# A planner's constants changed in a fused attention and gated-product kernel: a short wait for one engine, more places for raw weights, larger margins

## The chip, the cores and the metric

The kernel runs on one core of one Trainium2 chip. The metric is the device time of one execution in microseconds (us), as the median of several runs. A profile is one further execution, recorded by the hardware profiler.

## The reference

```python
# q, k, v: (8 batches, 8 heads, 576 tokens, 64); omega: (128, 64)
phi(x): h = x @ omega.T - sum(x*x)/2;  return exp(h - max(h)) / sqrt(128)     # x scaled by 64**-0.25
kv  = phi(k).T @ v;  z = sum over tokens of phi(k)
x   = (phi(q) @ kv) / (phi(q) @ z + 1e-6)                                      # -> (4608, 512)
out = ((x @ w_a) * (x @ w_b)) @ w_out                                          # w_a, w_b: 512 x 1536, w_out: 1536 x 512
```

q, k, v and omega are float32, the three weights come as float64.

## The kernel before

The work is cut by batch (8 of 576 tokens, of which 512 are the batch's main part; the 64 left over of every batch are gathered into a ninth block). For a batch there are four attention units, one for each pair of heads (`pair(u, gate)`, u = 4 * batch + pair), and then one block of gated products over 12 slices of the inner size 1536. A full-precision product is made of three passes over operands that are split into a high and a low part. Batches 0 and 1 use `moe_block` (L819 forms pa and pb, L774 forms the output o), the later blocks `moe_block7` (L909), which saves an eighth of the products with sums of weights that are made once, during batch 1, and kept in DRAM (`td`, `bd`).

Before the first block can run, the weights must be turned from 64-bit into two 32-bit parts. There are 36 weight units (for each slice one of w_a, one of w_b, one of w_out). For a unit, SyncE (SP) issues a load of 512 KB into a tile called `raw`; ACT runs two conversions on it (L319, L321); DVE joins them (L323); ACT or DVE makes the high part (L268 or L270), DVE the low part (L276). `raw` has a ring of two places of its own, raw0 and raw1. The first 18 units (n < 18) may also use the ten places in `late[:10]`, places of weights that are converted last and so are empty so far. The converted weights of slice i sit in 24 places w0..w11 and u0..u11.

No engine's order is the order in the source. `Graph` collects every operation with its dependencies, an estimate of its time, a priority (lower is earlier) and a `margin`; `schedule` then plays the whole program through on these estimates and writes down the order in which each engine is to work. On the chip the engines keep that order, whatever is late, and wait on semaphores. `need` is the earliest planned start: the end of the dependencies, a latency (70 ns, 150 ns more behind TensorE), plus `margin`, and not before `at` (for the conversion of unit n, 28000 + 2600 n ns). For every engine the planner takes the operation with the smallest key:

```python
o.need = max(t + o.margin, o.at)
...
key = (max(s, free[e] + 30), o.prio, o.n)
```

where `s` is the operation's earliest start and `free[e]` the time at which the engine is free. An operation that could start later than another that is ready loses, whatever the priorities are. Priorities: attention of pair u has 1000 u and a little more, so that the first batch lies below 4000; the conversion of unit n has 4000 + 111 n; copies and products of the block on DVE and ACT have -10.

In the first batch's attention (`tok_tail`) TensorE forms pn (L716), DVE adds, inverts, scales (`rd` L722 and L724, `x32t` L725, `tails` L729), twice for a pair, and TensorE transposes the result into px (L736). For most pairs of the later batches (27 in all) q' is scaled on ACT, transposed by DVE in blocks of 32 (`qd`), stored to DRAM by four DMAs (`qdr`, L633) and loaded back as `hq`; the load has `margin=CFG["BACK"]`. SP issues nearly all DMAs, in the planned order, and waits in that order.

Of the kernel before, what the change touches and what calls it, by code (L numbers as in the profile page):

```python
# [18 lines left out]
B, H, S, D, M = 8, 8, 576, 64, 128  # L19
# [14 lines left out]
SQ = (0.5 / float(D) ** 0.5) ** 0.5  # L34
EPS = 1e-6 * M

CFG = dict(FAST=(0, 1, 2, 3), JOIN0=False, WARM=8, HROOM=["w0", "u1", "w1", "u2", "w2", "u3"], H=3, TURN=(7,), BACK=300, AT=2, GATES=(-3, -1, 1, 3), SQPE=4, MARGIN=1200, LOAD=2500, SUMS=1000, JOIN=(0, 1, 2), CONV=(28000, 2600))

# [14 lines left out]
class Graph:  # L55
# [75 lines left out]
    def schedule(self, bw=330.0, dma_lat=2000):  # L131
        engines = ("PE", "ACT", "DVE", "POOL", "SP")
        free = dict.fromkeys(engines, 0)
        dma_free = 0
        after, left = {}, {}
        for o in self.ops:
            left[o] = len(o.deps)
            for d in o.deps:
                after.setdefault(d, []).append(o)
        ready = {e: [] for e in engines}  # L140

        def enter(o):
            t = 0
            for d in o.deps:
                same = d.eng.keys() == o.eng.keys() == {"PE"}
                t = max(t, d.end + (0 if same else self.LAT + (150 if "PE" in d.eng else 0)))
            o.need = max(t + o.margin, o.at)
            for e in o.eng:
                ready[e].append(o)

        for o in self.ops:
            if not left[o]:
                enter(o)
        done = []
        while len(done) < len(self.ops):
            best = None
            for e in engines:
                mine = None
                for o in ready[e]:
                    at = self.place(o) if o.alloc else (0, ())  # L160
                    if at is None:
                        continue
                    s = max(free[e], o.need, at[0])
                    for x in o.eng:
                        if x != e and max(free[x], o.need, at[0]) + o.eng[x] <= s + o.eng[e] - (o.eng[e] <= o.eng[x]):
                            break
                    else:

                        key = (max(s, free[e] + 30), o.prio, o.n)
                        if mine is None or key < mine[0]:  # L170
                            mine = key, s, o, at[1]
                if mine and (best is None or mine[1] < best[1]):
                    best = (*mine, e)
            if best is None:
                stuck = [o for e in engines for o in ready[e]]
                raise RuntimeError(f"stuck at {len(done)} of {len(self.ops)}: " + ", ".join(
                    f"{[b.name for b in o.alloc]}" for o in stuck[:12]))
            _, s, o, got, e = best
            o.start = s
            if o.bytes:  # L180
                free[e] = s + o.eng[e]
                begin = max(s, dma_free)
                dma_free = begin + o.bytes / bw
                o.end = dma_free + dma_lat
            else:
                o.end = s + o.eng[e]
                free[e] = max(s + 30, o.end - self.OVER[e])
            o.eng = {e: o.eng[e]}
            for b, slot in got:
                b.slot = slot  # L190
                self.slots[slot] = b
                self.rings[b.ring]["at"] += 1
            for r in ready.values():
                if o in r:
                    r.remove(o)
            done.append(o)
            for n in after.get(o, ()):
                left[n] -= 1
                if not left[n]:
                    enter(n)  # L200
        self.order = sorted(done, key=lambda o: (o.start, o.n))
        return self.order
# [11 lines left out]
def dve(n):  # L214
    return 150 + 1.04 * n


def act(n):
    return 165 + 0.86 * n
# [11 lines left out]
def tile_attention_moe(ctx: ExitStack, tc: tile.TileContext, kqt, kqtt, kqn, kqnt, vx, omst, idn, wab, wout, out):  # L231
    nc = tc.nc
    SQPE = CFG["SQPE"]
    const = ctx.enter_context(tc.tile_pool(name="const", bufs=1))
# [5 lines left out]
    def f(ap):  # L240
        return ap.bitcast(F32)

    g = Graph()
    for name, n in dict(X=2, Xw=0, nat=2, x2=0, v=2, h=CFG["H"], qd=1, kvz=1, sm=3, sq=3, ht=2, Xt=1, xl=0, xts=2, rd=2, x=4, xa=2, xf=2, S=2, st=0,
                        w=NF, u=NF, t=0, tst=0, wo=3, raw=2, a=2, c=0, bq=0, ghl=2, osb=0, zs=1, z2=1, zb=1, k2=1, kl=2, dn=1, tails=1, zr=1,
                        at=CFG["AT"], ab=2, o=4).items():
        g.ring(name, n)
# [16 lines left out]
    def copier(o, i, scale=None):  # L264

        def go(e):
            if e == "ACT":
                nc.scalar.copy(o(), i())  # L268
            elif e == "DVE":
                nc.vector.tensor_copy(o(), i())  # L270
            else:
                nc.gpsimd.tensor_scalar(o(), i(), 1.0, 0.0, op0=ALU.mult, op1=ALU.add)
        return go
# [13 lines left out]
    for k in range(4):  # L287
        g.op({"POOL": 110}, lambda e, k=k: nc.gpsimd.memset(ind.ap[D * (k // 2):D * (k // 2) + D, D * (k % 2):D * (k % 2) + D], float(k in (0, 3))),
             w=[(ind, k)], prio=-5000)
# [5 lines left out]
    def nothing(e):  # L295
        for _ in range(CFG["WARM"]):
            nc.tensor.matmul(none.ap[:], zero.ap[:], zero.ap[:, 0:1].to_broadcast([P, SM]), start=True, stop=True)
# [11 lines left out]
    def convert(raw, hi, lo, hb, n, pr, at):  # L309

        wd = (lambda: raw.ap.bitcast(I32).rearrange("p (n t) -> p n t", t=2)) if wide else None
        if wide:
            top, low = (lambda: wd()[:, :, 1]), (lambda: wd()[:, :, 0])

            g.op({"ACT": act(n) + 60}, lambda e: nc.scalar.activation(f(top()), f(top()), AF.Prelu, scale=2.0 ** -112, alpha=-2.0 ** 32),  # L319
                 r=[(raw, 1)], w=[(raw, 1)], prio=pr, at=at)  # L320
            g.op({"ACT": act(n) + 60}, lambda e: nc.scalar.activation(low(), low().bitcast(U32), AF.Copy, scale=2.0 ** -29 * 15 / 16),  # L321
                 r=[(raw, 0)], w=[(raw, 0)], prio=pr, at=at)
            g.op({"DVE": dve(n)}, lambda e: nc.vector.scalar_tensor_tensor(  # L323
                low(), top(), 3, low(), op0=ALU.logical_shift_left, op1=ALU.bitwise_or),
                r=[(raw, None)], w=[(raw, 0)], prio=pr, at=at)
            src = lambda: f(low())
        else:
            src = lambda: raw.ap[:, 0:n]
        g.op({"ACT": act(n) + 60, "DVE": 160 + 0.52 * n}, copier(hi, src), r=[(raw, 0)], w=[(hb, 0)], prio=pr, at=at, alloc=[hb])
        g.op({"DVE": dve(n)}, subber(lo, src, hi), r=[(raw, 0), (hb, 0)], w=[(hb, 1)], prio=pr, at=at)  # L330
# [5 lines left out]
    late = [f"{r}{k}" for k in range(NF - 1, -1, -1) for r in "uw"]  # L336
    for n, (kind, i, w) in enumerate(units):
        pr = 4000 + n * 4000 / len(units)
        more = late[:10] if n < 18 else []
        raw = g.buf("raw", [P, NW], I64 if wide else F32, f"raw{n}", more)  # L340
        src = (wab[i, w] if kind == "ab" else wout[i])
        g.op({"SP": 330}, dma(lambda raw=raw: raw.ap[:], lambda src=src: src), w=[(raw, None)], alloc=[raw], prio=pr - 600,
             nbytes=P * NW * (8 if wide else 4))
        if kind == "ab":
            hb = wab_b[i, w] = g.buf("wu"[i % 2], [P, 2, NC4, P], F32R, f"w{'ab'[w]}{i}")
            v = lambda hb, k: hb.ap[:, k].rearrange("p c f -> p (c f)")
        else:
            hb = wo_b[i] = g.buf("wo", [P, 2, E], F32R, f"wo{i}")
            v = lambda hb, k: hb.ap[:, k]
        convert(raw, lambda hb=hb, v=v: v(hb, 0), lambda hb=hb, v=v: v(hb, 1), hb, NW, pr, CFG["CONV"][0] + n * CFG["CONV"][1])  # L350
        if kind == "o":
            db = g.buf(None, None, None, f"wod{i}")
            wo_store[i] = db
            g.op({"SP": 330}, dma(lambda i=i: wod[i], lambda hb=hb: f(hb.ap)), r=[(hb, None)], w=[(db, None)], prio=pr + 600,
                 nbytes=P * 2 * E * 4)
# [75 lines left out]
    def square_sums(src, sq, n, nm, pr, b, alloc_sq):  # L431

        for nat, o, part in src:
            g.op({"ACT": act(n * D)}, lambda e, nat=nat: nc.scalar.activation(nat.ap[:], nat.ap[:], AF.Square, scale=SQ),
                 r=[(nat, None)], w=[(nat, None)], prio=pr, margin=0 if b < 2 else CFG["LOAD"])
            g.op({"DVE": dve(n * D)}, lambda e, nat=nat, o=o: nc.vector.tensor_reduce(o(), nat.ap[:], axis=X, op=ALU.add),
# [532 lines left out]
    for b in range(B + 1):  # L969
        if b < B1:  # L970
            moe_block(b)
        else:
            if b == B:

                for hp in range(NHP):
# [3 lines left out]
                         prio=-20, nbytes=P * SM * 4)  # L979
# [78 lines left out]
```

## Time and profile before

| what | us |
|---|---|
| median of 3 runs | 1091.68 |
| lowest and highest of them | 1089.23, 1092.51 |
| the profiled execution's own time | 1093.12 |
| its span from first to last instruction | 1091.3 |

The profiled execution took 1.8 us more than its span, and 1.4 us more than the median of the runs. In what follows PE is TensorE's matmul, PEld its weight load, DVE VectorE, ACT ScalarE, POOL GpSimd, SPq SyncE's DMA issues. A row of a timeline has the start, the duration, engine, line and operation, output<-input, and in brackets how long the engine was idle before it and what ended that. PE's busy time holds slow matmuls too: a matmul at a granted clock of 0.5 counts double.

### The profile page before, as it was taken

The numbers are of one execution on the slowest core, as the hardware profiler recorded it, in microseconds if no ns is written. First come the engines' busy times: TensorE is split into PE (matmuls) and PEld (weight loads), VectorE is DVE, ScalarE is ACT, GpSimd is POOL, SyncE is SP. The second block draws the span as 40 slices with busy tenths as digits, with TensorE's granted clock in tenths as the row PEclk, the third lists the DMA queues.
The fourth block names the chain that finished last, engine by engine and source line by source line (L and its number), as shares of the span: only waits on it lengthen the run. The fifth ranks groups of instructions, "written<-read, shape, count | busy, mean of one in ns | idle before, by whom it ended". The sixth has DMA issues, their size and how long they took to land.

```text
span 1091.3 us, 21360 instructions
## 1 busy us (share of the span) xinstructions
PE 1071.8 (98%) x7725; PEld 928.2 (85%) x7725; DVE 802.7 (74%) x1975; ACT 575.5 (53%) x1557; POOL 102.9 (9%) x176
## 2 busy tenths in 40 slices
PE   8999899999999999999999999999999999999998
PEld 7877677777779888988888989888898989999997
DVE  5899687889897778777696888777876766456544
ACT  6987667767674556564565566464645412002001
POOL 0011111111010111110111111010101100000000
PEclk9989999999999999999999999999999999999999
DMA  9656765798779788978889798888786798777773
GB/s 360 231 201 189 247 226 192 260 324 300 260 280 364 266 285 307 322 275 287 279 289 324 258 301 279 311 278 290 262 306 225 251 288 284 243 241 256 258 233 88
DMA packets 113209, 292.45 MB, mean 268 GB/s; under 512 B 16208, under 2 KB 33360, under 8 KB 113104
## 3 DMA queue, kind: packets, MB, share of 16 engines
q1 hardware_dynamic: 112496, 290.44, 78.4%
q8 instruction: 61, 1.00, 0.4%
q10 hardware_dynamic: 608, 0.66, 0.2%
q14 instruction: 44, 0.36, 0.1%
HBM read 242.61 MB, written 48.43 MB: 267 GB/s over the span
## 4 chain that ended last, share of the span: by engine, by line
PE 83%; DVE 6%; DMA 4%; ACT 3%; issue 1%; SPq 0%; ACTq 0%; DVEq 0%
PE p L909 37%; PE o L774 25%; PE ppk L449 5%; PE pb L819 4%; PE pa L819 4%; PE pkv L584 3%; PE pm L643 2%; DMA out_dram<-osb 1%; DMA raw<-in_wab_dram 1%; ACT hq L615 1%; DVE raw L323 1%; DVE sm L470 1%; DMA td<-ts 1%; DVE c L919 1%; DMA hq<-qdr 1%
## 5 line engine op out<-in xcount | busy, mean ns | idle before, releaser
L774 PE MATMUL o<-wo,ghl 128*128 128x512 f32 x1296 | 352.7, 400 | 0.3 <-ACT osb L268 0.2
L919 DVE TENSOR_TENSOR c<-p,c 128x512 f32<-128x512 f32 (+1 forms) x336 | 208.1, 619 | 141.8 <-PE p L909 139.5
L774 PEld LDWEIGHTS o<-wo,ghl 128*128 128x128 f32 x1296 | 225.7, 189 | 41.3 <-ACT osb L268 0.7
L909 PE MATMUL p<-S,t 128*128 128x256 f32 x1512 | 208.8, 283 | 0.7 <-ACT c L268 0.7
L909 PEld LDWEIGHTS p<-S,t 128*128 128x128 f32 x1512 | 195.7, 190 | 9.3 <-ACT c L268 1.5
L551 POOL TENSOR_TENSOR z<-hk 128x256 f32<-128x256 f32 x56 | 44.2, 789 | 714.9 <-ACT hk L482 684.0
L482 ACT ACTIVATE hk<-hk,sm 128x128 f32<-128x128 f32 x192 | 63.1, 394 | 56.1 <-DVE sm L478 53.9
L268 ACT COPY c<-p 128x256 f32<-128x256 f32 x84 | 31.0, 369 | 109.8 <-PE p L909 105.6
L615 ACT ACTIVATE hq<-hq,dn 128x128 f32<-128x128 f32 x224 | 70.3, 395 | 33.4 <-DVE dn L611 32.7
L268 ACT CAST ghl<-c 128x512 fp32r<-128x512 f32 x54 | 33.3, 621 | 92.0 <-DVE c L954 90.4
L605 DVE CUSTOM_DVE_ANT_0 junk<-hq,zb 128x128 bf16<-128x128 f32 x224 | 65.2, 291 | 17.8 <-ACT zb L268 15.6
L449 PEld LDWEIGHTS ppk<-om,X 64*128 64x128 f32 x512 | 61.9, 188 | 18.7 <-issue 6.2
L449 PE MATMUL ppk<-om,X 64*128 64x128 f32 x512 | 74.0, 285 | 2.6 <-DVE x L276 2.3
L819 PE MATMUL pb<-x,wb 128*128 128x512 f32 x288 | 76.3, 405 | 0.0
L909 PEld LDWEIGHTS p<-x,t 128*128 128x128 f32 x504 | 70.3, 189 | 6.8 <-DVE c L919 0.3
L449 PE MATMUL ppq<-om,X 64*128 64x128 f32 x512 | 73.7, 285 | 0.7 <-ACT kl L268 0.7
L819 PE MATMUL pa<-x,wa 128*128 128x512 f32 x288 | 74.0, 401 | 0.0
L909 PE MATMUL p<-S,bq 128*128 128x256 f32 x504 | 73.9, 282 | 0.0
L909 PE MATMUL p<-x,t 128*128 128x256 f32 x504 | 73.9, 282 | 0.0
L909 PEld LDWEIGHTS p<-x,wb 128*128 128x128 f32 x504 | 65.4, 188 | 4.3 <-DVE zr L276 0.3
L909 PEld LDWEIGHTS p<-x,wa 128*128 128x128 f32 x504 | 65.1, 188 | 4.3 <-DVE c L919 0.6
L909 PE MATMUL p<-x,wb 128*128 128x256 f32 x504 | 68.1, 282 | 0.0
(158 smaller groups left out, 1713.1 us busy)
## 6 DMA issues: line engine op xcount, KB each, us to landing
t<-td SPq DMA_DIRECT2D x168, 512.0 KB, 5.2
wo<-wod SPq DMA_DIRECT2D x96, 512.0 KB, 5.3
bq<-bd SPq DMA_DIRECT2D x84, 256.0 KB, 5.4
X<-in_kqt_dram SPq DMA_DIRECT2D x31, 512.0 KB, 5.5
qdr<-qd SPq DMA_DIRECT2D x108, 144.0 KB, 3.5
hq<-qdr SPq DMA_DIRECT2D x27, 576.0 KB, 6.6
raw<-in_wab_dram SPq DMA_DIRECT2D x24, 512.0 KB, 5.0
td<-ts SPq DMA_DIRECT2D x24, 512.0 KB, 5.5
```

The lines of the kernel that those rows point to most:

```text
L268: nc.scalar.copy(o(), i())
L449: nc.tensor.matmul(pps[w].ap[:, c * M:c * M + M], x()[rows, c * P:c * P + P], om.ap[rows], start=True, stop=True)
L482: g.op({"ACT": 392}, lambda e, c=c, w=w: nc.scalar.activation(dst[w].ap[:, c], src[w](c), AF.Exp, scale=SC, bias=sm.ap[:, 2, w, c:c + 1]), ...
L551: g.op({"POOL": pool2(n)}, lambda e: ENG[e].tensor_tensor(o(), a(), c(), op=ALU.add), r=r, w=w, alloc=list(al), prio=pri)
L584: nc.tensor.matmul(pkv.ap[D * j:D * j + D, 0:M], vb.ap[:, vc, 0:D], c(), start=(n == 0), stop=(n == 4))
L605: g.op({"DVE": 413}, lambda e, c=c, j=j, rr=rr, qc=qc: nc.vector.tensor_tensor_reduce(out=junk.ap[rr], in0=qc(), in1=zb.ap[rr, j], scale=1 ...
L615: g.op({"ACT": 392}, lambda e, c=c, src=src: nc.scalar.activation(hq.ap[:, c], src(), AF.Copy, scale=dn.ap[:, c:c + 1]), r=[sd, (dn, None) ...
L643: nc.tensor.matmul(pm.ap[D * j:D * j + D], kl.ap[:, j], qT[1](j), start=True, stop=True)
L774: nc.tensor.matmul(po.ap[:], ghl.ap[:, gi, t * P:(t + 1) * P], wo.ap[:, wi], start=(n == 0 and i == 0), stop=(n == NF - 1 and i == 2))
L819: nc.tensor.matmul(pb.ap[:], wt.ap[:, wi, c], xs[c].at(xi), start=(c == 0 and i == 0), stop=(c == NC4 - 1 and i == 2))
L909: nc.tensor.matmul(pb.ap[:, half], wcol(wi, c), xc(xi, c), start=n == 0, stop=n == 5)
L919: g.op({"DVE": dve(n)}, lambda e: nc.vector.tensor_tensor(c4.ap[:, o], pb.ap[:, half], y(), op=ALU.add), r=[*((pb, k) for k in range(half. ...
```

## The change

Four constants of the plan change. DVE's key may treat an operation of the first batch's attention (priority 0 to 4000) that can start up to 150 ns after DVE is free as if it were ready, so that its priority decides. The two ACT conversions of a raw tile get a margin of 2000 ns behind the planned landing of its load. The margin of the load of q' goes from 300 to 1500 ns. And raw tiles of units 18 to 23 may use six further places, of units 24 to 29 three, of units 30 to 32 one, where they had only raw0 and raw1. The instructions are the same; their order, the places and the waits follow from a new plan.

```diff
-CFG = dict(FAST=(0, 1, 2, 3), ... BACK=300, ... CONV=(28000, 2600))
+CFG = dict(WAIT=150, RAW=2000, FAST=(0, 1, 2, 3), ... BACK=1500, ... CONV=(28000, 2600))
...
-                        key = (max(s, free[e] + 30), o.prio, o.n)
+                        wait = CFG["WAIT"] if e == "DVE" and 0 <= o.prio < 4000 else 0
+                        key = (max(s - wait, free[e] + 30), o.prio, o.n)
...
             g.op({"ACT": act(n) + 60}, lambda e: nc.scalar.activation(f(top()), f(top()), AF.Prelu, scale=2.0 ** -112, alpha=-2.0 ** 32),
-                 r=[(raw, 1)], w=[(raw, 1)], prio=pr, at=at)
+                 r=[(raw, 1)], w=[(raw, 1)], prio=pr, at=at, margin=CFG["RAW"])
             g.op({"ACT": act(n) + 60}, lambda e: nc.scalar.activation(low(), low().bitcast(U32), AF.Copy, scale=2.0 ** -29 * 15 / 16),
-                 r=[(raw, 0)], w=[(raw, 0)], prio=pr, at=at)
+                 r=[(raw, 0)], w=[(raw, 0)], prio=pr, at=at, margin=CFG["RAW"])
...
-        more = late[:10] if n < 18 else []
+        more = late[:10] if n < 18 else late[:6] if n < 24 else late[:3] if n < 30 else late[:1] if n < 33 else []
```

## Rows read from the trace of the kernel before

**Rows 1.** The page's head and its first part: busy us, share, instructions.
```profile
span 1091.3 us, 21360 instructions
...
PE 1071.8 (98%) x7725; PEld 928.2 (85%) x7725; DVE 802.7 (74%) x1975; ACT 575.5 (53%) x1557; POOL 102.9 (9%) x176
```
**Rows 2.** TensorE's waits, whole span: engine, line, releaser: us, times, longest.
```profile
PE px L736 <- DVE x32t L725: 3.1, 1, 3.1
PE pk L594 <- ACT hk L482: 2.8, 1, 2.8
PE ppk L449 <- DVE x L276: 2.3, 2, 2.0
PE pm L643 <- DMA hq<-qdr: 1.0, 1, 1.0
...
PE ppq L449 <- ACT kl L268: 0.7, 1, 0.7
...
PE o L774 <- ACT osb L268: 0.2, 1, 0.2
```
**Rows 3.** Windows: length, PE, PEld, DVE, ACT, POOL busy, PEclk, DMA share, GB/s.
```profile
56.30:63.20 6.90, 6.26 (x27) 4.67 (x28) 5.34 (x11) 3.71 (x10) 1.20 (x2) 0.51 0.57 205
...
124.60:128.00 3.40, 3.03 (x9) 2.00 (x9) 1.12 (x2) 2.75 (x9) 1.64 (x3) 0.50 0.51 167
128.00:300.00 172.00, 168.89 (x1000) 131.21 (x1000) 147.10 (x377) 120.33 (x315) 25.13 (x36) 1.00 0.76 257
```
**Rows 4.** Timeline of PE around 54 us.
```profile
51.35 2.48 PE L716 MATMUL pn<-kvz,qT 128*128 128x100 f32 x20
56.94 1.09 PE L736 MATMUL px<-ident,x32t 128*128 128x128 f32 x4 [3.12 <-DVE x32t L725]
```
**Rows 5.** Timeline of DVE, two chains from pn to x32t.
```profile
32.55 0.16 DVE L722 TENSOR_SCALAR rd<-pn 128x5 f32<-128x5 f32 x1 [0.73 <-PE pn L716]
...
32.98 0.42 DVE L725 TENSOR_TENSOR x32t<-pn,rd 128x256 f32<-128x256 f32 x1
...
53.78 0.15 DVE L722 TENSOR_SCALAR rd<-pn 128x5 f32<-128x5 f32 x1
53.85 0.68 DVE L323 SCALAR_TENSOR_TENSOR raw<-raw 128x512 int32<-128x512 int32 x1
...
55.39 0.67 DVE L276 TENSOR_TENSOR wa<-raw,wa 128x512 fp32r<-128x512 f32 x1
...
56.39 0.41 DVE L725 TENSOR_TENSOR x32t<-pn,rd 128x256 f32<-128x256 f32 x1
```
**Rows 6.** Timeline of DVE, SP and ACT, 111 to 141 us.
```profile
111.47 0.68 DVE L276 TENSOR_TENSOR wb<-raw,wb 128x512 fp32r<-128x512 f32 x1
...
112.22 0.33 SPq L279 DMA_DIRECT2D raw<-in_wab_dram  x1
...
119.19 0.67 ACT L319 ACTIVATE raw<-raw 128x512 f32<-128x512 f32 x1 [4.23 <-DMA raw<-in_wab_dram]
...
140.48 0.67 ACT L319 ACTIVATE raw<-raw 128x512 f32<-128x512 f32 x1 [2.61 <-DMA raw<-in_wab_dram]
```
**Rows 7.** SP's waits, whole span.
```profile
SPq L279 <- DMA qdr<-qd: 18.5, 27, 3.1
```
**Rows 8.** Tile raw, whole span: its instructions (ns min/median/max), loads to landing.
```profile
L323 DVE SCALAR_TENSOR_TENSOR raw<-raw x36: 650/685/1232, 35.3 to 178.2; 128x512 int32<-128x512 int32 x36
...
L270 DVE CAST wo<-raw x12: 414/425/684, 45.4 to 178.9; 128x512 fp32r<-128x512 f32 x12
L276 DVE TENSOR_TENSOR wo<-raw,wo x12: 678/684/1107, 46.6 to 179.3; 128x512 fp32r<-128x512 f32 x12
...
DMA to landing us min/median/max: 3.4/4.7/10.0
```
**Rows 9.** Windows of 27.3 us, columns as above.
```profile
54.60:81.90 27.30, 24.96 (x143) 19.38 (x144) 24.58 (x51) 22.81 (x56) 3.83 (x6) 0.87 0.59 200
81.90:109.20 27.30, 27.20 (x130) 21.45 (x129) 26.09 (x82) 20.25 (x52) 3.84 (x6) 1.00 0.60 190
```

More of the change, by code (lines that the diff above doesn't have):

```diff
@@ L35 @@
 EPS = 1e-6 * M
-CFG = dict(FAST=(0, 1, 2, 3), JOIN0=False, WARM=8, HROOM=["w0", "u1", "w1", "u2", "w2", "u3"], H=3, TURN=(7,), BACK=300, AT=2, GATES=(-3, -1, 1, 3), SQPE=4, MARGIN=1200, LOAD=2500, SUMS=1000, JOIN=(0, 1, 2), CONV=(28000, 2600))
+CFG = dict(WAIT=150, RAW=2000, FAST=(0, 1, 2, 3), JOIN0=False, WARM=8, HROOM=["w0", "u1", "w1", "u2", "w2", "u3"], H=3, TURN=(7,), BACK=1500, AT=2, GATES=(-3, -1, 1, 3), SQPE=4, MARGIN=1200, LOAD=2500, SUMS=1000, JOIN=(0, 1, 2), CONV=(28000, 2600))
 class Buf:
```

## The prediction

> **What bounds the kernel now.** I read the page's first part, then TensorE's waits, then windows for the granted clock, then the timelines around the long waits. PE is busy for 1071.8 of 1091.3 us [rows 1], so TensorE sets the time: its work stays, and only what it loses can be won back. It loses two things. The first is waiting: twelve lines, 14 waits, together 14.0 us, from 3.1 us for px down to 0.2 us for o [rows 2]. The second hides inside the busy time: in 56.3 to 63.2 us and in 124.6 to 128.0 us the granted clock is about a half [rows 3], the lower of its two levels (1.2 for 2.4 GHz), so that half of 6.9 and of 3.4 us of work is loss, 3.4 and 1.7 us. Each stretch begins inside one of the two waits near 3 us (px, which ends at 56.94 [rows 4], and pk); behind the 2.0 us wait of ppk, which lies in 128 to 300 us, the clock stays at 1.00 [rows 3]. A wait of 3 us thus costs TensorE about twice its length. After 300 us PE is busy nearly throughout and nothing there is worth more than the 1.0 us that pm waits for q' [rows 2]. So the stage in which the change can work is the first 150 us.
>
> **The wait of DVE (A).** pn ends at 51.35 + 2.48 = 53.83; px starts at 56.94 [rows 4]. Between them DVE has to add, invert and scale. Undisturbed, that took from 32.55 to 32.98 + 0.42 = 33.40, 0.85 us, for the same three instructions in an earlier pair [rows 5]. Here it took from 53.78 to 56.80, because a join (L323, 0.68) and a low part (L276, 0.67) of weights, and smaller things, stand between the links [rows 5]. The order is the plan's: a link that becomes ready some 0.1 us after DVE is free loses to a ready conversion. With 150 ns of grace it wins, and the chain closes up. pn's second half ends last, so px could start at 53.83 + 0.85, some 54.7: a wait of 0.9 in place of 3.1. One conversion of 0.68 may still be running when the first link gets ready, so I take 1.6. Gained: 1.5 us. The wait is then shorter than the 2.0 us that left the clock alone, so the low stretch should go too, 3.4 less the 0.2 to 0.3 that lies inside the wait: 3.2 us. A together 4.7. Its bounds: 0, if the link's lateness is over 150 ns or another plan puts something else there; and 3.1 + 3.2 = 6.3.
>
> The price of the grace: DVE stands idle for up to 0.15 us at a link. Two pairs of the first batch remain when conversions begin at 28 us by plan; by the code each has some twelve such DVE instructions, so at most 24 x 0.15 = 3.6 us of DVE time, by my reckoning a third of it. What is late next are conversions. They are covered: none of TensorE's twelve waits is put down to a converted weight [rows 2]. Were that cover gone, it would be up to 3.6 us at the end of the stage.
>
> **The places for raw tiles (B, C).** From unit 18 on there are two. At 111.47 DVE makes the low part of a unit, at 112.15 it is done, at 112.22 SP issues the next load into that place, and ACT, whose next planned instruction is that unit's conversion, stands idle for 4.23 us until 119.19; the same for 2.61 us before 140.48 [rows 6]. Behind the conversion in ACT's order stand the exponentials of an attention pair, hk, for which TensorE's pk then waits 2.8 us, and after the second one kl, for which ppq waits 0.7 us [rows 2]. With eight places for units 18 to 23, five to 29 and three to 32 a load is issued that many units ahead. At the plan's 2.6 us for a unit that is 20.8, 13.0 and 7.8 us against landings of 3.4 to 10.0, 4.7 in the middle [rows 8]: the load is there. The margin of 2000 ns does the rest: a conversion is planned after its load even if that takes 2 us longer. The last three units keep two places, and there a wait like the old one stays possible; TensorE then has other work, I put it at nothing, at most at one wait of 2.8. The loads move forward in SP's queue, 0.33 us of issue each [rows 6], past the loads of X, q and k; they no longer hold SP up for a place. DMA share there is 0.59 and 0.60 [rows 9], so the transfers find room. B: 2.8 of waiting and 1.7 of clock, less 0.2 that is in both, 4.3. C: 0.7. Bounds of both together: 0, if ACT is held there by something else, and 5.0.
>
> **The margin of q'.** Each of 27 reloads makes SP wait for the store, 18.5 us in all, 3.1 at most [rows 7]. With 1.2 us more the plan lets other loads go first, and q' comes up to 1.2 later. TensorE has waited for q' once, 1.0 us [rows 2]; its products are planned later by as much. I take nothing, with 1.0 won and 1.2 lost as ends (once, since the other 26 reloads had slack). The 2.3 us of ppk I leave as they are.
>
> **The sum.** A new plan makes new small waits. The old one has 14 waits of 1.0 us on average [rows 2]; I add one, +1.0. Then -4.7 - 4.3 - 0.7 + 0.0 + 1.0 = -8.7 us. Against the execution's own 1093.1 that is 1084.4; the median of the runs lies 1.4 below that execution, so I forecast 1083.0 for the median. Likeliest case: 1080 to 1087, from the sum with A at 6.3 and no new wait (-11.3) to the sum with A at 2 and two new waits (-5.0).
>
> A rule that speaks against the clock terms stands in the Trainium skill, "TensorE: Matmul & The Clock Gate", section "What's actually happening": how many matmuls run slowly differs from run to run of one kernel. If so, the two low stretches say little of other executions; no trace here shows a second one. By it the sum would be without the two clock terms, which is the fourth rival below.
>
> **The rivals.** Times are on the execution's scale, then on the median's.
> First, A stays: DVE has other work at hand all the time, and a plan shifted by a few hundred ns may put other work between the links, which the grace does not see when a link is later than 0.15. Then the change does not do there what it says: -4.3 - 0.7 + 1.0 = -4.0, 1089.1, 1087.7: still just faster. For it: DVE is busy for 24.6 of 27.3 us there [rows 9]. Against: three links take 0.85 us in all when undisturbed, 0.16 and 0.42 of it the first and the last [rows 5], so the gaps between them are short.
> Second, the waits move: a new plan gives one more wait of the px kind, 3.1 + 3.2 = 6.3, elsewhere: -8.7 + 6.3 = -2.4, 1090.7, 1089.3, within 0.3%. For it: the old plan had two such in 130 us.
> Third, slower: DVE becomes the bound. Six more places let six units be converted earlier, into 54.6 to 109.2 us. A unit costs DVE 0.69 + 0.68 + 0.42 = 1.8 us [rows 8], six 10.8; DVE has 2.7 + 1.2 = 3.9 us free there [rows 9]. The other 6.9 push an attention chain back, TensorE waits that long with B's and C's gain gone, and the clock falls as at px: -4.7 + 1.0 + 6.9 + 3.2 = +6.4, 1099.5, 1098.1. It decides for slower as soon as more than 0.5 us reaches TensorE, and beyond 3.8 us by more than 0.3%. Against it: conversions have later priorities than the block's and the earlier pairs' work, so they should take only idle places.
> Fourth, the clock falls all the same, in stretches of the same length elsewhere: -8.7 + 3.2 + 1.5 = -4.0, 1089.1, 1087.7.
>
> **How the numbers follow.** Forecast 0.42, first rival 0.14, second 0.20, third 0.17, fourth 0.05, nothing changes at all 0.02. Differences under 0.3%, 3.3 us, can't be told from none here: the three runs shown span that much. Faster: 0.42 + 0.14 + 0.05 = 0.61; same 0.22; slower 0.17. The range: at the lower end all of A to C at their upper bounds with ppk's 2.0 and pm's 1.0 won and no new wait, -6.3 - 5.0 - 2.0 - 1.0 = -14.3, 1078.8 and 1077.4, so 1077; at the upper end it holds the second rival and the bound of "same", 1095, and a little of the third: 1096. That leaves out some 0.17.
>
> **What would show it.** In the changed profile: px waits under 1.7 us and no conversion stands between the links from pn to x32t; no window before 150 us with a granted clock below 1.00; ACT's waits for raw loads (6.8 us in rows 6) under 2; SP's waits for the store of q' well under 18.5, and pm still at 1.0 or less. The prediction is wrong if TensorE's waits before 200 us still add up to 8 us or more, or if a new one near 3 us shows up with a low clock behind it, above all one put down to DVE between 54 and 130 us.

## The result and the profile after

| | us |
|---|---|
| median of four runs of the changed kernel | 1076.72 |
| lowest and highest of them | 1074.46, 1077.46 |
| the kernel before, four runs beside them | 1091.8 |
| the profiled execution's own time, and its span | 1077.46, 1075.7 |

The ratio is 0.9859, with an interval of 0.9839 to 0.9878: 15.1 us or 1.4% faster. I had forecast 8.7 us less and 1083.0; the measured median lies 0.3 us below the range. The direction and the place were right, the size was not.

All line numbers of the changed kernel are higher by two from the old L169 on. The page's head, its first part and the granted clock in 40 slices (tenths of full speed) answer to [rows 1]:

```profile
span 1075.7 us, 21363 instructions
...
PE 1064.4 (99%) x7725; PEld 925.3 (86%) x7725; DVE 804.4 (75%) x1980; ACT 572.1 (53%) x1552; POOL 103.0 (10%) x176
...
PEclk9999999999999999999999999999999999999999
```

The number of matmuls is the same, and yet TensorE's busy time fell by 7.4 us: busy time holds slow matmuls too. The windows, with the columns of [rows 3, 9], say where:

```profile
54.60:81.90 27.30, 26.70 (x167) 20.29 (x167) 27.08 (x52) 25.24 (x61) 4.55 (x7) 1.00 0.88 304
81.90:109.20 27.30, 27.30 (x146) 22.20 (x144) 26.39 (x86) 23.43 (x57) 1.94 (x3) 1.00 0.59 198
...
56.30:63.20 6.90, 6.82 (x34) 4.84 (x36) 6.87 (x15) 6.50 (x18) 0.97 (x1) 1.00 0.93 313
124.60:128.00 3.40, 3.40 (x32) 2.48 (x33) 2.37 (x5) 2.86 (x8) 2.06 (x3) 1.00 0.99 320
128.00:300.00 172.00, 171.91 (x1019) 133.09 (x1015) 151.62 (x402) 120.74 (x319) 22.39 (x36) 1.00 0.80 269
```

Both low stretches are gone. From 54.6 to 81.9 us TensorE starts 167 matmuls where it started 143, and DVE, third in the row, is busy for 27.08 of 27.30 us instead of 24.58. TensorE's waits answer to [rows 2]:

```profile
PE p L911 <- ACT c L270: 1.1, 2, 0.9
PE o L776 <- ACT osb L270: 1.1, 1, 1.1
PE none L299 <- DVE zero L294: 1.0, 1, 1.0
PE pk L596 <- ACT hk L484: 0.5, 1, 0.5
...
PE pm L645 <- DMA hq<-qdr: 0.5, 1, 0.5
```

px is no longer among them; pk has come down from 2.8 to 0.5; ppk with its 2.3 is gone as well. All waits together are 5.8 us where they were 14.0. Around the old wait for px the timeline of PE, and below it that of DVE, answer to [rows 4, 5]:

```profile
51.33 2.37 PE L718 MATMUL pn<-kvz,qT 128*128 128x100 f32 x20
53.48 0.93 PE L821 MATMUL pb<-x,wb 128*128 128x512 f32 x3
...
55.43 0.65 PE L738 MATMUL px<-ident,x32t 128*128 128x128 f32 x4
```
```profile
52.62 0.17 DVE L724 TENSOR_SCALAR rd<-pn 128x5 f32<-128x5 f32 x1 [0.20 <-PE pn L718]
...
53.74 0.17 DVE L724 TENSOR_SCALAR rd<-pn 128x5 f32<-128x5 f32 x1
53.94 0.19 DVE L726 RECIPROCAL rd<-rd 128x5 f32<-128x5 f32 x1
54.16 0.42 DVE L727 TENSOR_TENSOR x32t<-pn,rd 128x256 f32<-128x256 f32 x1
...
54.94 0.69 DVE L325 SCALAR_TENSOR_TENSOR raw<-raw 128x512 int32<-128x512 int32 x1
```

Two things differ from before. On DVE the first link now stands at 52.62, behind 0.20 us in which DVE waits for pn: that is what the grace plans. The links of the pair's two halves follow each other, and the join comes behind them. On TensorE the plan has put three products pb, and then phi's small products, between pn and px, so that px does not wait at all, although x32t is done only at 54.58. ACT's waits for raw loads, SP's for the store of q' (answering to [rows 6, 7]) and the joins (as in [rows 8]):

```profile
ACT raw L321 <- DMA raw<-in_wab_dram: 3.4, 1, 3.4
ACT raw L321 <- DMA raw<-in_wout_dram: 1.6, 1, 1.6
...
SPq L281 <- DMA qdr<-qd: 16.5, 23, 3.0
```
```profile
L325 DVE SCALAR_TENSOR_TENSOR raw<-raw x36: 677/686/699, 36.4 to 162.1; 128x512 int32<-128x512 int32 x36
```

The last join starts at 162.1 us; it started at 178.2.

**Where the time came from.** I took the start times of all 7725 matmuls in both traces. The gap between two starts, less the usual gap behind a matmul of that line, counts as lost where it is over 20 ns; so waits and low clock are both in it. The rest is the usual gap itself, which is compared by its mean.

| stretch | lost before, us | lost after, us | difference |
|---|---|---|---|
| up to the block's first product | 5.9 | 5.9 | 0.0 |
| block of batch 0 | 19.1 | 8.1 | -11.0 |
| block of batch 1 | 9.5 | 6.5 | -3.0 |
| later blocks, first half | 21.0 | 23.2 | +2.2 |
| later blocks, second half | 7.0 | 6.5 | -0.5 |
| usual gap: L909 (256 columns) 118.21 to 117.66 ns, 3528 times | | | -1.9 |
| usual gap: L774 (512 columns) 233.3 to 232.2 ns, 1296 times | | | -1.5 |
| sum | | | -15.7 |

The last matmul starts 15.7 us earlier (1086.0 and 1070.3). By start times alone, the usual gap included, the five stretches changed by +0.2, -11.8, -3.3, +0.9 and -1.7 us; with its last two rows shared out, the account agrees with that within 0.6 us. No step of the prediction has the two terms of the usual gap.

### The profile page after: what moved, and what is told of

The parts are those of the page before. It is cut to its first block, busy times and chain, and to the rows that moved or that the text cites. A ratio compares the mean times of both kernels' runs of the same rounds, so it can differ in the third digit from the quotient of the medians.

```text
span 1075.7 us, 21363 instructions
## 1 busy us (share of the span) xinstructions
PE 1064.4 (99%) x7725; PEld 925.3 (86%) x7725; DVE 804.4 (75%) x1980; ACT 572.1 (53%) x1552; POOL 103.0 (10%) x176
## 4 chain that ended last, share of the span: by engine, by line
PE 85%; DMA 5%; DVE 5%; ACT 1%; issue 1%; SPq 0%; ACTq 0%; DVEq 0%
PE p L911 36%; PE o L776 25%; PE ppk L451 5%; PE pb L821 5%; PE pa L821 5%; PE pkv L586 3%; DMA out_dram<-osb 2%; PE pm L645 2%; DVE sm L472 1%; DMA hq<-qdr 1%; DMA td<-ts 1%; PE ppke L451 1%; DVE raw L325 1%; DMA raw<-in_wab_dram 1%; DMA wo<-wod 0%
## 5 line engine op out<-in xcount | busy, mean ns | idle before, releaser
L270 ACT CAST ghl<-c 128x512 fp32r<-128x512 f32 x50 | 31.0, 622 | 83.4 <-DVE c L956 81.6
L821 PE MATMUL pb<-x,wb 128*128 128x512 f32 x288 | 74.7, 400 | 0.0
L821 PE MATMUL pa<-x,wa 128*128 128x512 f32 x288 | 74.2, 400 | 0.1
L911 PE MATMUL p<-x,wb 128*128 128x256 f32 x504 | 68.7, 283 | 0.0
```

The costliest lines, as they stand in the source:

```text
L821: nc.tensor.matmul(pb.ap[:], wt.ap[:, wi, c], xs[c].at(xi), start=(c == 0 and i == 0), stop=(c == NC4 - 1 and i == 2))
L911: nc.tensor.matmul(pb.ap[:, half], wcol(wi, c), xc(xi, c), start=n == 0, stop=n == 5)
```

## The experiments

**One part alone, on the kernel before.** Each kernel takes a single constant of the change.

```diff
# alone_wait:   CFG ... WAIT=150
# alone_places: more = late[:10] if n < 18 else late[:6] if n < 24 else late[:3] if n < 30 else late[:1] if n < 33 else []
# alone_raw:    CFG ... RAW=2000
# alone_back:   CFG ... BACK=1500
```

> Only DVE's grace of 150 ns. Theory 1 (each part takes away the wait that it aims at, and the parts add up): the wait of px (3.1 us) and the low-clock stretch behind it (6.9 us at half rate, 3.4) go, the raw-load waits near 119 us stay: ratio 0.994 (-6.5 us). Theory 2 (any new plan shakes the long waits off, the gains do not belong to parts): px's wait may or may not go, and so may pk's near 125 us; ratio anywhere from 0.985 to 1.003.

> Only the further places for raw tiles. Theory 1: ACT's waits for raw loads (4.2 and 2.6 us) go, with them pk's 2.8 us, ppq's 0.7 and the low-clock stretch from 124.6 us (1.7): ratio 0.9955 (-5 us); px's wait of 3.1 us and its low clock stay. Theory 2: px's wait changes as well. Theory 3 (the margin of 2000 ns is what frees ACT, not the places): ACT still waits for loads 5 us or more and the ratio is 1.000.

> Only the margin of 2000 ns behind the landing of raw loads, with two places from unit 18 on. Theory 1: conversions come later, TensorE's work is ordered around them; ACT's waits for loads shrink but the conversions are still paced by two places: ratio 0.998 to 1.003. Theory 3: ACT's waits and pk's go: ratio 0.9955.

> Only the margin of q', 300 to 1500 ns. Theory 1: nothing before 100 us changes, so px's and pk's waits with their low clock stay; pm's 1.0 us goes, and the 2.3 us of ppk near 226 us may: ratio 0.997 to 1.000. Theory 2: 0.99 to 1.003.

| kernel | median, us | ratio to before, interval | what is left in its trace |
|---|---|---|---|
| alone_wait | 1083.26 | 0.9901, 0.9873 to 0.9930 | px waits for nothing, no low clock anywhere; ACT waits 16.7 us for raw loads, pk 2.0 |
| alone_places | 1085.53 | 0.9927, 0.9905 to 0.9950 | px 3.1 and the low clock behind it; pk gone |
| alone_raw | 1093.25 | 1.0000, 0.9980 to 1.0019 | px and its low clock; pk gone; pm 3.6 |
| alone_back | 1093.82 | 1.0009, 0.9992 to 1.0025 | px and its low clock; pk 1.6; p<-c 3.2 |

The grace alone gives two thirds of the gain, the places alone half of it, the margins nothing. (Of the 9.1 us by which alone_wait's last matmul starts earlier, 3.5 are a shorter usual gap; the other three have the gap of before.) alone_wait shows that a raw wait of ACT does not by itself bring a low clock: ACT waits longer for loads than before,

```profile
ACT raw L321 <- DMA raw<-in_wab_dram: 8.4, 4, 4.1
ACT raw L321 <- DMA raw<-in_wout_dram: 8.3, 3, 4.5
```

and still no stretch has a low clock. It does not show that such waits are free: pk still waits 2.0 us, in two pieces instead of 2.8 in one. alone_places keeps the old chain at px, first its row in the timeline, then the window behind it, with the clock at a half:

```profile
56.81 1.08 PE L736 MATMUL px<-ident,x32t 128*128 128x128 f32 x4 [3.14 <-DVE x32t L725]
...
56.00:62.80 6.80, 5.99 (x27) 4.41 (x28) 5.24 (x11) 3.88 (x10) 1.24 (x2) 0.50 0.97 352
```

The start of the same product pa or pb can be compared between kernels, best where the orders of the plans agree again. From the 100th to the 140th product of the block, the changed kernel is 5.4 us ahead of before, alone_wait 5.3, alone_places 0.2. So the 5.4 belong to the grace. By the 200th alone_places is 6.0 ahead and the changed kernel 11.6. The two margins alone gain early too (alone_raw is 6.6 us ahead at the 200th product, without the places) and give it back by waits that the new plan makes later.

**One part taken back, on the changed kernel.**

```diff
# no_wait:   CFG ... WAIT=0
# no_places: more = late[:10] if n < 18 else []
# no_raw:    CFG ... RAW=0
# no_back:   CFG ... BACK=300
```

> The changed kernel without DVE's grace. Parts alone measured: grace 0.990, places 0.993, margin of raw 1.000, margin of q' 1.001; the whole 0.986. Theory 1 (the grace owns px's wait and its low clock): both are back, ratio 0.993. Theory 2 (any new plan shakes the waits off): px waits under 2 us without the grace and the ratio is under 0.990.

> The changed kernel with two places from unit 18 on, the margins and the grace kept. Theory 1 (places own the second gain): ratio 0.990, as with the grace alone, conversions again run until about 180 us. Theory 3 (the 2000 ns margin frees ACT just as well): ratio 0.986 to 0.988, ACT waits under 4 us for raw loads.

> The changed kernel without the 2000 ns behind raw loads. Theory 1: with places ahead the loads have landed, the margin is worth nothing: 0.986 within 0.3%. Theory 3: ACT waits for loads again as in the kernel before, 6 us or more, and a wait near 3 us with low clock is back: 0.990.

> The changed kernel with 300 ns behind the store of q'. Theory 1: nothing in the first 100 us differs and TensorE waits little for q' either way: 0.986 within 0.3%, pm's waits up by 0.5 to 1.5 us. Theory 2: anywhere between 0.983 and 0.992.

| kernel | median, us | ratio to before, interval |
|---|---|---|
| no_wait | 1089.72 | 0.9959, 0.9944 to 0.9973 |
| no_places | 1089.14 | 0.9963, 0.9944 to 0.9982 |
| no_raw | 1085.18 | 0.9928, 0.9904 to 0.9952 |
| no_back | 1082.70 | 0.9899, 0.9874 to 0.9925 |

Taken back, the four parts cost 10.9, 11.4, 7.5 and 4.4 us by these ratios, 34 us together, where the whole change gained 15; put in alone, they gained 10.8, 8.0, 0.0 and -1.0. So the parts don't add up, and three of these four ratios lie outside what either theory expected: each constant sets a new plan.

Without the grace px waits 3.1 us again, with the clock at 0.50 from 57.7 to 61.1 us, and pm waits 3.0. Without the places the conversions come too late for the products, first TensorE's waits, then the windows behind them:

```profile
PE o L776 <- DVE wo L272: 2.2, 1, 2.2
PE o L776 <- DVE wo L278: 1.8, 2, 1.2
...
155.20:158.60 3.40, 3.40 (x19) 2.55 (x19) 3.11 (x13) 1.49 (x3) 0.00 (x0) 0.50 0.86 224
172.20:175.60 3.40, 2.86 (x7) 2.28 (x8) 3.33 (x6) 2.03 (x6) 0.78 (x1) 0.50 0.45 91
```

That is the cover that I had named for the grace (converted weights are there in time) giving way. alone_wait, with the grace and two places but without the margins, has no such waits for wo, so it is the margins that need the places; that it is the 2000 ns and not the margin of q' is likely, but no run separates them. no_raw gets a wait of ppq (1.8) and a low stretch at 325.7 us behind a wait for c; no_back gets pm 2.8 and ppk 1.9 and no low stretch.

**The DVE chain by itself.** If closing the chain from pn to x32t is what the grace does, moving only those instructions by hand in the order of before should give A's 5.4 us. links_moved puts the DVE links of the last pair right behind what they depend on; links_free also moves two reductions (L470) behind them.

```diff
+    for o in [o for o in order if "DVE" in o.eng and o.prio in (3130, 3140)]:
+        order.remove(o)
+        last = 1 + max(last, *(order.index(d) for d in o.deps))
+        order.insert(last, o)
...
# links_free, behind it
+    for o in [o for o in order if "DVE" in o.eng and o.prio in (4000, 4001) and any("PE" in d.eng for d in o.deps)]:
+        order.remove(o)
+        order.insert(last, o)
```

> The kernel before with its own plan; only DVE's order around px is edited by hand: the four links of each half (add, invert, scale, tails) of the first batch's last pair stand right behind what they need, everything else on every engine keeps its order. Theory 1 (A is worth its wait and its low clock): px's wait falls from 3.1 to 0.9-1.6 us, no low-clock stretch at 56 us, ratio 0.9945 (-4.7 to -6.3 us). Theory 2 (most of the grace's -10 us comes from the other orders of a new plan): not more than that here, so the grace's further 4 to 5 us is the new plan's. Theory 4 (the grace's full -10 us is the chain): 0.990.

> The kernel before with its own plan; on DVE the links of the last pair right behind what they need, and the two reductions of the next batch (which held the second half back) behind them. Theory 1: px waits 0.9 to 1.2 us and the clock stays up, ratio 0.9955 to 0.996 (what the late link cost the changed kernel, 4 us, is won here). Rival (the wait is only passed on): px's wait gone, another near it, ratio above 0.998.

Measured: links_moved 1094.02, ratio 1.0010 (0.9992 to 1.0028); links_free 1093.86, 1.0009 (0.9994 to 1.0025). Neither won anything. links_moved, its wait and the window behind it:

```profile
PE px L736 <- DVE x32t L725: 2.0, 1, 2.0
...
57.60:64.40 6.80, 6.23 (x25) 4.51 (x24) 6.67 (x14) 5.68 (x16) 1.65 (x2) 0.50 0.59 188
```

px waits 1.1 us less, and the clock falls all the same, for 6.8 us. The chain is closed here only within each half of the pair; between the halves DVE still makes the two reductions:

```profile
54.28 0.67 DVE L470 TENSOR_REDUCE sm<-ppk 128x4 f32<-128x512 f32 x1
54.88 0.67 DVE L470 TENSOR_REDUCE sm<-ppq 128x4 f32<-128x512 f32 x1
55.48 0.15 DVE L722 TENSOR_SCALAR rd<-pn 128x5 f32<-128x5 f32 x1
```

links_free:

```profile
PE ppke L449 <- ACT hk L482: 2.1, 1, 2.1
...
PE px L736 <- DVE x32t L725: 1.0, 1, 1.0
...
59.60:63.00 3.40, 3.40 (x17) 2.92 (x18) 3.37 (x7) 2.68 (x6) 0.78 (x1) 0.50 0.28 54
```

Here px is down to 1.0 us, and 1.7 us after its start TensorE stands for 2.1 us at phi's products, which wait for ACT's hk: hk is made from sm, which comes out of the reductions that were pushed back. The wait was passed on, not won. Two premises of step A fall: a closed chain is not enough, and a wait of 2.0 us does not leave the clock alone as such.

**The price of the wait.** late_link is the changed kernel with ten memsets on DVE ahead of the last pair's second add; they write what x32t overwrites later, so it computes the same.

```diff
+            def first(e, j=j, o=o, pn=pn, rd=rd):
+                if hp == 3 and j == 1:
+                    for _ in range(10):
+                        nc.vector.memset(x32t.ap[:, :, 1], 0.0)
```

> The changed kernel with its own plan and orders; ten extra clears of a 128x256 piece on DVE (about 3 us, no change to the result) stand ahead of the last pair's second add, so px is late again. Theory 1: TensorE waits some 2.5 to 3 us there, the clock falls to a half behind it, and the whole is 4 to 6.5 us longer than the changed kernel: ratio to before 0.990 to 0.992. Rival: a wait at one place is taken up later, where TensorE waits less: ratio 0.986 to 0.988.

Measured: 1080.33, ratio 0.9896 (0.9864 to 0.9928). The row of px in the timeline (the lines from there on are four higher than in the changed kernel), and the window behind it:

```profile
58.14 1.11 PE L742 MATMUL px<-ident,x32t 128*128 128x128 f32 x4 [2.70 <-DVE x32t L731]
...
57.20:64.00 6.80, 5.86 (x16) 4.45 (x17) 6.33 (x15) 3.51 (x8) 0.91 (x1) 0.50 0.53 171
```

The wait and the low clock are back, and cost 4.6 us by the 100th product and 3.1 us at the last one. That is step A's price, put in by itself. By whole times it is 4.0 us, but the interval overlaps that of the changed kernel (up to 0.9878), and the slowest of the four executions, 1083.17, had a mean granted clock of 1.00: there the low stretch did not come.

**Neighbouring plans.** back_1700 and raw_2200 change one margin of the changed kernel by 200 ns.

```diff
# back_1700: CFG ... BACK=1700
# raw_2200:  CFG ... RAW=2200
```

> The changed kernel with 1700 ns in place of 1500 behind the store of q'; a neighbouring plan, whose orders differ from some 100 us on. If the 15 us come from the parts (theory 1): 0.986 within 0.3%. If a good part is this plan's luck behind the first 150 us (theory 2): up to 0.993.

> The changed kernel with 2200 ns in place of 2000 behind the raw loads; a neighbouring plan. Theory 1: 0.986 within 0.3%. Theory 2: up to 0.993, with px's wait and the low clock in the first 150 us gone all the same, and the loss in small waits later.

Measured: raw_2200 1077.40, 0.9866 (0.9841 to 0.9891), like the changed kernel. back_1700 1084.51, 0.9930 (0.9902 to 0.9958). Its first 240 products are as far ahead of before (11.9 us) as those of the changed kernel (11.5). Then come waits for c (2.6 us) and for ghl (1.5), and one low stretch:

```profile
315.80:319.20 3.40, 3.10 (x14) 3.10 (x15) 0.55 (x3) 0.80 (x2) 0.00 (x0) 0.50 0.94 291
```

So the first 160 us are the change's doing; what happens to 0.7% of the time behind them depends on the plan as a whole, and 200 ns of a margin can turn it.

**The usual gap.** The pool gives a tile its address in SBUF when the plan first uses it, so a new plan gives other addresses. old_plan_new_places has the order of before and the changed kernel's addresses, new_plan_old_places the reverse: tiles are created ahead, in the other kernel's order.

```diff
+    PLACES = 'u11 w11 u10 v0 ... k20 ...'.split()     # the slots in the wanted order
+    for s in PLACES:
+        sp.tile(first[s].shape, first[s].dtype, tag=s, name="first_" + s)
```

new_plan_sorted_places has the changed plan and an order of the slots by which every t lies 224 bytes over a multiple of 256. all_places puts the w and bq there too; t_beside_s puts t there, and S and x, the moving tiles of its products, as well, where the others have them at 160.

> The kernel before with its own plan and orders; only the addresses in SBUF are those that the changed kernel's tiles got (31 of 76 places lie elsewhere). Theory 5 (in every kernel with the grace a product of L909 and L774 takes 0.5% less time because its tiles lie elsewhere): L909's products start 117.7 in place of 118.2 ns apart, L774's 232.1 in place of 233.3, whole ratio 0.997 (-3.4 us). Rival (the rate hangs on the plan, on what the other engines do meanwhile): ratio 1.000.

> The changed kernel with its plan, on the addresses of the kernel before. Theory 5: products at 118.2 and 233.3 ns, ratio 0.989 (3.4 us given back). Rival: 0.986 as the changed kernel.

> The changed kernel with its plan; the five places of t all at addresses that leave 224 by 256, both of ghl at such that leave 160, as the quicker ones did so far (t 115.7 to 117.2 ns at 224, 118.7 at 160 or 32; ghl 231.5 at 160, 233.0 at 224). If that is what tells them apart: 2.5 ns less for three fifths of the t products and 1.5 for half of L774's, 3 to 4 us, ratio 0.9825. If it is chance: 0.986 and rates between 115.7 and 119 for the places of t as before.

> The changed plan as it is, with only the tiles in SBUF placed by hand: every t, every w and the bq tiles at addresses that leave 224 over multiples of 256, and S, X, xa, the wo and ghl at ones that leave 160. In the kernel whose t alone are placed so, products with t as the stationary tile followed each other every 115.2 to 115.6 ns, the others of L909 every 118 to 119. If the address of the stationary tile by itself sets the spacing, the w and bq products come down by some 2.5 ns as well: some 2.5 us less than in new_plan_sorted_places (1072.15), ratio near 0.979. If it was a chance of those places, or belongs to the pair of tiles, no gain on it: ratio 0.981 or above.

> The changed plan, t at addresses that leave 224 over multiples of 256 as in new_plan_sorted_places, but S and x, the moving tiles of the same products, at 224 as well, and wo and ghl at 160. If the absolute address of the stationary tile sets the spacing, products with t stay near 115.4 ns and the ratio near 0.9815. If what counts is how the addresses of the stationary and the moving tile stand to each other, products with t go back to some 118.7 ns and the ratio to about 0.986, that of the changed kernel.

The mean gap is that from one product of L909 (256 columns) to the next, worked out from start times.

| kernel | median, us | ratio to before, interval | mean gap, ns |
|---|---|---|---|
| old_plan_new_places | 1090.31 | 0.9979, 0.9962 to 0.9996 | 117.66 |
| new_plan_old_places | 1078.98 | 0.9870, 0.9847 to 0.9893 | 118.18 |
| new_plan_sorted_places | 1072.15 | 0.9814, 0.9792 to 0.9837 | 116.25 |
| all_places | 1071.18 | 0.9801, 0.9783 to 0.9819 | 115.48 |
| t_beside_s | 1079.24 | 0.9881, 0.9865 to 0.9898 | 118.75 |

The gap goes with the addresses and not with the plan; so does that of L774, 232.1 ns in old_plan_new_places and 233.2 in new_plan_old_places. All kernels here with the grace and addresses of their own have a gap of 117.6 to 117.7 ns, all without the grace one of 118.2. The groups of instructions by line and shape show it without any working out; the numbers are the instructions, their busy time, and the mean ns of one. The products of S and t, in turn of before, the changed kernel, new_plan_sorted_places and t_beside_s:

```profile
L909 PE MATMUL p<-S,t 128*128 128x256 f32 x1512 | 208.8, 283 | 0.7 <-ACT c L268 0.7
```
```profile
L911 PE MATMUL p<-S,t 128*128 128x256 f32 x1512 | 208.2, 283 | 1.1 <-ACT c L270 1.1
```
```profile
L911 PE MATMUL p<-S,t 128*128 128x256 f32 x1512 | 204.4, 280 | 1.7 <-ACT c L270 1.6
```
```profile
L911 PE MATMUL p<-S,t 128*128 128x256 f32 x1512 | 210.1, 284 | 1.2 <-ACT c L270 1.1
```

The same 1512 products take 204.4 us in one layout and 210.1 in another of the same plan. By the remainders of the two addresses to 256, for products with t as the stationary tile:

| t, moving tile | kernel | gap, ns |
|---|---|---|
| 160, 160 | before | 118.9 |
| 32, 160 | after | 118.8 |
| 224, 160 | before, after, new_plan_sorted_places, all_places | 117.1, 116.0, 115.1, 114.9 |
| 224, 32 | new_plan_sorted_places | 117.7 |
| 224, 224 | t_beside_s | 119.1 |

The last row decides between the two theories: with t at 224 the gap is long again when the moving tile lies at 224 too. For t it is the pair of addresses that counts, not the stationary tile's own. The remainders are no general rule, though. In L774 (ghl stationary, wo moving) the equal pair is the short one: 160 and 160 give 231.5 ns, 224 and 160 give 232.8 to 233.3. And in all_places, where every pair of L909 is 224 and 160, the products with w still take 117.3 ns. Its bq products went from 118.6 and 115.0 in new_plan_sorted_places to 113.7 and 114.5 ns, while those with w moved little (67.3 and 68.7 us for 504 each to 67.1 and 68.4). Its ratio lies between the two figures that were expected; 1.0 us under new_plan_sorted_places is less than the intervals can tell. Both beat the changed kernel.

## Why the prediction was right and wrong

**The steps that failed.** The prediction began with TensorE's work that "stays", so that only waits and low clock could be won back. The work did not stay: the same matmuls followed each other at a shorter usual gap, and that gave 3.4 us, for which the sum has no term. And "The 2.3 us of ppk I leave as they are" put the block of batch 1 at nothing, where 3.0 us were won. The two make 6.4 of the 7.0 us between -8.7 and -15.7. The lower end of the range, -14.3, held ppk's 2.0 us but not the gap; with it the end would have been near 1074. Within the steps, A had its size from a mechanism that did not hold.

**The place was right.** TensorE's waits and the low clock before 150 us were the loss, and they went. The block of batch 0 gained 11.0 us by the account above, where A, B and C had 4.7 + 4.3 + 0.7 = 9.7. What was to be seen: no conversion between the links, px under 1.7 us, no clock below 1.00 before 150 us, pm at most 1.0, all so. ACT's raw waits were to be under 2 us and are 5.0; pk waits only 0.5 us all the same, and alone_wait had no low clock with 16.7 us of such waits. SP's waits for the store of q' were to be well under 18.5 and are 16.5: I had taken the other loads to go first, and mostly they don't.

**Step A had the size and not the mechanism.** 4.7 forecast, 5.4 and 5.3 measured by the 100th product, 4.6 put back there by late_link. But the step took the rows at 53.78 and 56.39 [rows 5] for one chain. They belong to the two halves of a pair, and besides the conversions two reductions hold up the first half:

```profile
52.59 0.68 DVE L470 TENSOR_REDUCE sm<-ppk 128x4 f32<-128x512 f32 x1
53.19 0.68 DVE L470 TENSOR_REDUCE sm<-ppq 128x4 f32<-128x512 f32 x1
...
55.32 0.15 DVE L722 TENSOR_SCALAR rd<-pn 128x5 f32<-128x5 f32 x1
```

It also said that closing the chain does it, and that a wait of 1.6 or 2.0 us leaves the clock alone. links_moved closed the chain in part and links_free closed it whole, and neither won anything. What the new plan has besides is filler on TensorE between pn and px and an order in which hk is not pushed back; that these two make the difference is read from the timelines, no run has the one without the other. The clock's price was a little high, too: at 0.50 products of 512 columns start 427 ns apart, where L821's start 232 apart at 1.00, so that not half but 46% of a low stretch is loss, by this estimate 3.1 of 6.8 us. A grace in a planner is not a local edit: it sets a new order on every engine.

**Steps B and C were right in kind.** By the 200th product alone_places had won 5.8 us over its lead at the 140th, where 5.0 were forecast. But alone_raw was as far ahead there without the places, and pk's wait is not steady: it is 1.5 us at the same place in old_plan_new_places, which has the orders of before. What the runs show of the places beyond that is that with them the gain was kept: alone_raw's last matmul starts 0.4 us later than that of before. Over the whole kernel places alone gave 0.9927, and without them the changed kernel loses 11.4 us (0.9963 against 0.9859), more than the 5.0 I had as upper bound. The excess is the price of the margins without places (no_places): waits for converted weights, which I had called covered.

**"The 2.3 us of ppk I leave as they are" failed.** The block of batch 1 gained 3.0 us, most of it that wait at 226 us. It went in alone_wait and alone_places too, each with an order of its own; which instruction it was that moved is not isolated.

**The margin of q' at nothing holds alone** (alone_back 1.0009). Within the new plan it is open: no_back lies 0.4% above the changed kernel with intervals that just touch, and back_1700 0.7% above. Those are changes of the whole plan behind 160 us, not of q' alone. The same spread is what my "one new wait, +1.0" was for; the changed kernel paid +1.7 there, and back_1700 lies another 7.8 us above it (1084.51 against 1076.72).

**No step had the usual gap.** 3.4 us of the 15.7 came from tile addresses. By whole times the swap of addresses gave 0.21% (0.04 to 0.38) in the old plan, which holds 3.4 us; in the new plan 0.9870 against 0.9859, which the intervals don't tell apart. That the gap depends on the layout is shown by new_plan_sorted_places and t_beside_s, whose intervals lie apart.

In sum: -9.7 forecast for block 0 and -11.0 measured; 0 and -3.0 for block 1; +1.0 and +1.7 behind them; 0 and -3.4 for the gap.

**The rivals.** A stays, and the waits move: neither. DVE as the bound: it came close, with 27.08 of 27.30 us busy from 54.6 us on, yet TensorE waited for nothing of it; the bound of 0.5 us that was to decide was not reached. The clock falls all the same: not in the changed kernel. The rule behind that rival stands in the Trainium skill, "TensorE: Matmul & The Clock Gate", section "What's actually happening": of the slow matmuls at a kernel's start it says that their number differs from run to run. The low stretches here are like that in part. In all eight profiled kernels in which px waits 2.0 us or more a low stretch follows it, 6.8 us long in seven of them and 3.4 in no_wait. But old_plan_new_places, with the orders of before, has its second low stretch at 140.9 us and not at 124.6. And the mean granted clock of the executions of the kernel before goes from 0.991 to 0.998, which at a clock of 0.50 is, by my estimate, 20 down to 4 us of low clock in one execution. So the two clock terms of the sum, 3.2 and 1.5 us, were those of one execution. The changed kernel's four executions have 0.999 or 1.00.

## What to carry to other kernels

When a planner's constant changes, price the first stage from its waits, and then give the rest a term for the new plan itself: here its neighbours differ by up to 0.7% behind the stage that was meant. A wait closed by hand is won only if the engine finds work in the gap and what was pushed back is not what it needs next, so look for the filler and for the next releaser before counting the gain. Before comparing two plans, hold the tile addresses equal, or compare the gap between like matmuls first: two layouts made for one plan lay 0.7% apart here.

## What the runs showed of the hardware that was not expected

- The gap from one matmul to the next depends on where its two operands lie in SBUF: 114.9 to 119.1 ns for the products with t (256 columns, the same instructions). There 224 for the stationary and 160 for the moving tile (over multiples of 256) was short, equal remainders (160 and 160, 224 and 224) long. For L774 (512 columns) it was the other way round, 231.5 ns at 160 and 160 and 232.8 to 233.3 at 224 and 160, and for w 224 and 160 was not short (117.3). Why, and why 224 with 160 still ranges from 114.9 to 117.1 for t, stays open; 256 is only the number by which the addresses were sorted, and no run moved one tile by itself.
- The length of one wait doesn't say whether the granted clock falls behind it. After 2.0 us for px in links_moved it was 0.50 for 6.8 us, after 1.7 us for c in no_raw 0.50 for 3.4 us, and in links_free, after waits of 1.0 and 0.7 us for phi's products near 139 us, 0.50 for 3.4 us; after the 2.0 us wait of ppk before [rows 2, 3] and the 1.8 us of ppq in no_raw it stayed at 1.00.
